# Q and K weights loaded three heads at a time, with another order of the work at both ends

## The chip, the cores and the metric

The kernel runs on one core of a Trainium2 chip. The metric is the device time of one execution in microseconds (us). Engine names are those of the profile: PE multiplies matrices, PEld loads its weights, DVE and ACT do elementwise work, POOL and SP mostly issue DMAs, POOL also small computations.

## The reference

Two kinds of layer, each run twice, A, B, A, B, on x of 2048 rows by 512, all in bf16:

```python
for s in range(n_seg):                     # 64 segments of 32 rows
    h = concat([mem, xs])                  # 8 rows of memory, 32 of the segment
    q, k, v = h @ Wq, h @ Wk, h @ Wv       # 32 heads of 128
    p = softmax(where(mask, q @ k.T * scale, -1e9))
    o = (p @ v) @ Wo
    mem = o[:8]; outs.append(o[8:])        # the memory goes on to the next segment
...
h = sigmoid(g) * u                         # B: g, u, down projection, F = 1792
```

Each layer takes a layer norm first and adds its input behind it. A starts from the same mem0 and the same weights both times. So the segments of one A are a chain: segment s + 1 needs the memory that segment s gives.

## The kernel before, in words

**Steps.** Both A layers run in one loop of 70 steps (emit_step). Step t does segment t of the first A layer and, beside it in the same matmuls, segment t - 6 of the second. The first six steps and the last six therefore have one layer alone (40 columns in a matmul, and not 80). Four segments are a block of 128 rows; when a block has left the first A layer, its B layer (ffn, lines 1048 to 1150) runs between the steps, and so on for the second. A step goes through 6 head groups: heads 0 to 2 and 16 to 18, then 3 to 5 and 19 to 21, and so on to 15 and 31. Per group: Q and K (L892), scores (L906), the softmax on DVE and ACT (L920 to L937), transposes (L949), P times V (L975), and the output projection (L993) into one PSUM bank for all groups. The next step needs the memory columns from that bank, copied at L1011.

**V.** V of the rows of x is not made in the steps. A V pass (v_pass, lines 686 to 711) takes 128 rows, makes V for eight pieces of 512 columns with four matmuls each (L695; I call these four a V piece), copies each out of PSUM, and stores it to a scratch tensor in DRAM; a step fetches its rows from there (L861). Seven passes at the start, 56 V pieces, serve ten blocks (v_group); their copies go to nine staging buffers, which are the B layer's weight tiles, not needed yet. A half pass (v_half, L732, stores at L746) and a strip (L817) do the same for a part of a block. In every step a strip makes V of the 8 memory rows and a few rows of x.

**Loads at the start.** All weights stay in SBUF. load_weights (lines 582 to 614) issues them on SP's queue: Wv in 8 pieces of 4 heads, the x of nine blocks between them, then Wq, Wk and Wo. Wo comes by head group. Wq and Wk come in pieces that start at heads 0, 3 and 9 (and 16, 19 and 25) and hold 3, 6 and 7 heads. In DRAM a head has 256 B in each of 512 rows, so a piece of m heads is 512 rows of 256 m bytes.

**What sets the order.** Each operation is a task with its engine, cost and keys read and written (Planner.add). SEQUENCE, a compressed list in the file, gives each task its place: at each moment an engine takes, of the tasks that are ready in a model of the chip, the one with the lowest place (forward, lines 272 to 413). What comes out is the program's fixed order on each engine; on the chip every engine takes its queue in order. Tasks that may run on either of two engines (copies on ACT or DVE, the boot stores on SP or POOL) get the one that is free first in the model. Where the model sees PE idle at either end, filler matmuls on a tile of zeros (L1218) go in.

Of the kernel before, what the change touches and what calls it, by code (L numbers as in the profile page):

```python
# [53 lines left out]
;Ag)rXk7pcfB%7A@!gH@5PER9zwFwU*Txh6(FIfkX|(7J?i&Gymhh!kX3<9*It9&+^ANuZ3nQF%vjb@k;)ADNDw~7A&yK6rftjYT<(0_Cu$F5_QL}_k&+#M$g4fMAuI3%VR%9II^4edG>hLecVFKKZ  # L54
fiq<zaDy4oUFv58J8W8}M`2{oi5UUb^!f*Ro0Ll?vc4MO@r^c`&wF^g&x{e8(wi=&1jnm{X}@GBNB?B98ftnN@q;Urg_TN7gRljNIZ1xL04!;{jd2yH$?cL&EwR4Y4Tqu8pK|P3tu<gW{h$`ab{UE_
fqK5_Bs&J*b^6-QBtiB1Rm-Zu8Nlc!2f&|gEyzQ&Zou|%s7^3{5zh9KTUR}tya8Oc6!P`{0)Vq8I;Cl`Bjt~AjrB%)CqD@z82Z2w;QrC0`{pXpx_R2Wh&&#2H3QIv3WnP|a@1!GQgacw;pKW^M`R|!
Nk+QQ;DjyYF5GF7!M*<sd8cVD>2uHyj70Z$6aD8lSDtqSMB#M+!9iZef2n{|jXj7clA2G^EzqM!g-lB)@}v+s<dLTg#Kii~);*dJP_OtPjOrD`dCRS`B*?af^G#|5&z)YMf)|%^UO;YbIwUZ94H|;|
&I8kZBVH%Vr|M`z4VQLMuW2mhCo%WGrCP@C3|aBQ!Z@sF?{dn1nHiX-Hcv2SE;6gPREA8v1gxUN5fjwov7s7E=){nUleMkl)rSwf-#NWnt+iLb)vYQSg8NO|ck6a&f5J`jCYy?w$`JBYrP7VoA#kkX
>yw8_VzTSGOpj8yq?_x;;hBH;rz~q4SdF9ZBg{rG@)htW>FtF!fG!q1a8hR)S^e6}q?Lzs^}+^#ob7fH!>Fyt6Ec%(XxD2g=*h~t0x*|HYIgpYBcJ&io_?o{l)`4GU_@%j@)8o~)(WjyR`I-_DVdEX
qpsq`mM61>+(8TaM-5>9Drz=jnb)-=yYKy|4I>K@zHNw@rcCC|=f*ye&WaMflMV5|xPNyTb*H)NgH9?jw1M*`|Aqy&^a*rUk;3mH)kGJznF1RvY3@t@=2^xaH0-f1Ty6gB5>G7cN@NTPLrchUmPhHP  # L60
BPzZ2ia}YU1q5^?Zh`JV^|-uLP^j5y#P_ZT06?ozV2jLQSp96AT@omT@9`T$m-yy@g4kD5^7&#?)KvIhz5<IDDn_B}S$w_%O54$*Uf&%*f!G9A0k)w2S80jRm_OzzD}%&|JCO=Jux2;jsV1&&*ocDe
vv19OW<}n=z=BXtevuQth?wJcFw3v~A;KU0Fj8U7v;-ubd1)6$LvOp^(EF2YN4lWzA>9UsIioM@psu~u&Horxi#{K)nGF~9<5jCnBT^6l!UsB(k4o)!8A~I>f8#r%yu%<R0mYyTfZ<)Sni2UT(vn0#
tm2cI5k@+Ojklj8V{nBRX$UB+gfBzr^hrH>$u5kX5;NqVjvk?&E^!9Un709~&!yGdZ`zS12GJ~~o>$PW0_Q(~(ech%@Dd4F?a@?s&4w?B3X^B#o>$WuxPHlU8E1h;6sRCPM;Cb&M89tcFI3Fc7SaL-
@ko8IZK`J@W2GEGmX}g(7vDTBKpV{0l0Fa*zKW5nQtSNYScG9m-W4oihEpRM9oZhx$s8@o43g~=;)6hTN^z^Shvggyiw$J(S&trHsZko5QCciufS!$?n=$+iEW_#~(`j}&V4WCWgYlK!d#Qs8!?9zj
+bqOxo_kt*eZ7rE@04&B0z8Nz9i<d40QttTz6^4LDi~8yhg8P4NzvULMSQJ-$b!TRs-7IAd_l8GT;#XHgZcX$-$b)HgDh{d9p!Ey5NK#kZ(Nzsu&svhey17&ct5)NozyL<4jW>hTpOmDH`UV?uNeKn
ulL27>(f<<fI2lD7P@{ZxKK5izxo4o_!^ec%pEaQr`~plAyRxTVWrISSzr8X5TfH(1GV1AzqFJC@ZL5V(+q2z_(&=mUZDhaes!D&m_4JvmfF?Tb1D<p2^ZH$QTP$`?ht%YJSK>L&CcqNEJ<!Kr{4oz
vj+K3Emf<Ch%)`ULp{|Z!2<pl7r@(XMSkbViiH_g;!i$l%ewSb&20V3maX%pZQ9=^qZ9wc+A{sGfKnIIgZi9N`Aj$1&p0a=tUVPau*9x6O+3z+=cQwW#v2L`O$oZv0t|=^q0+3wovlZqw;CjluSfY1
7;)b2dM;AEItw!IJo9aZVFG>~c1D!+Q8oJ6gHCVjgh+q=g5RV7n;S4Z{Vb-#GBbB5;S`h<JtFjk*+%dBbL|0-RP<JoBUp$?mRdco7QSmHHji-UX7~{&TCk0xhlix|OcNZzn$a?dwXxy6toswR3nCxg
<$l)jDf(|Z9;2QA2Pa?Sr*59(v?!>Gw*!qSrriD#k;zlQ3O)3BertDQxc3{@%R7C#_YLB_AsNpEq&sbpzKmH~RYP~bk{Zd_?;Wo1EPM{r9g$C}>3;0X_dxzhSf2(<dWtt@E+CAb_+p>QbPZxM{{PS3
*en5KD&!3JofsA3^5fe+Yc=aOqR)fM<|mNjpQ}L_L`b6F5Z9!0Ny_KiYa1f=>UfHv5NT}Dt#)}&@tB}*TmVzJN!1wQ308W#%Ewt9=zute@fBG_bJI~rE8@x(8H9zT)JiPkVik)hOISJpJ`Z|aqfuxS  # L70
9MY^{ThVokOpd=UmpouWZAyJ+>Q&s<TSe0J7BeE=BIr=gLszKqR~2v6Y6>hu2k+cm^UC_1#1b|?t!P7;XyfV~lp@ZnPb$}EWnWzg)_Pm2Q2jbtP7fuO#3di=k)6Dpo<n|F!K`{GgUY<TL&xEiPlsLE
&`&N90i`ZrB`F!^X2xQ#Z*X7g10f8gpm<n@MdGTPU@}*SmWq{(s7(9g_Cv(?{N1{2oaF^jfe$o_VK4qMF^xSK*{cee3e$;(u_$eW`lc&g&EI&y4i*uW%6zw-NX1hb(pOJBbt)zq^a*_i4QZU3OsA`a
ogk8T2n3iX4#2Ol?c4h;A1AqM9wA^Jr*lL?l6X!W4a}idB0|TS{P^F0xoo=H?n}?x#S)J57?AP`%qwl>;dln_?FWE@z$Yf>Vqz`|dwyR1uaTh&cJ&l`kd!X_?-X)Uh(;|b$81Dn>eA?1v=O~yq6@bR
lvtg%>-}E)I4o%t7|qUp0K%C@$IO_3Q8c<f2sy?3NQKPEsTbru3QRD|F$a4d@f{&HJW`|O6+dZE$zQ(5B{Er!7rj;f4B;-AE4MX{;f6HfmZJze6(XM=l9u^A_U!OD95{V?ww{=>wQP72Z~s4Qm*vR?
e*y&gf*;_)**=M^LbI7dC46mRe<kfr+>_l^QZ>lm(OXgC(MLi@qI+N!-8i=oU4&L8DE2q;wf%=IK%<}jzPwj}l6xHHB!-gZcv^HoZ{V!;w_?ExVSCPsDrsA{#Sb51#5b-20&?c^99>Nt=R8W4MSi*l
MCgAULe{=wE<IiLPE}6f&Z9CBTjxxm#$_7R6;Z-ebVg&LO>WXD!Pep6L3A0rMfMW?E%7v;VO`&f|Ap|wZ??;v^Q~wr_4FD&tZm<<vV<O6&>j+yJH$*U-MCo}`YUh|$58?UEU%S|;`YMe5WJlSWE_kL
E)LRM0MQ6r<a(5C^kO>B<W_mrR)FViX&=9@G;RSwumdZ&Qt1(0oIO6ak`3nRTF(wTL^pIe!t#dYVm=<rx<3Qr+huU{k!&q2AKPMS@{}fFPJPOl#O~xT)AjxxLZv|mhvohJ9z}-?!-FGN&=ldq)4r!D
*cp!V%Xw+RfahwLc)Ig{IHF)!SEG<NE#(9Yjhv#WJHTKEisY~5+qr=eRZhP)FaoF64N_9o35pnE(v8PoEVgW0r7x!jM^tenC7jjy!)MB3AcYWC48j5cMuv^}G6mD{UWyge2qtcY@;VQVZW$|axO~Oh
vJ(=-Q@Ew*P=dF|XXgO7`vJ<K48cKaSn5!FbYSw;t|wilbDVKhl?<VuNKghUS_lENW9>r$n!HW<BYwx!DFqn}AM7hQA@+s#m*u9N`b@Ma9m(V@dcecx`>pXpHMrdvT!$c6$7K*gPb#>jO6SUnwQF@S
>&t@I)gR?aZ}gYOy@|#4pu_GanAT5qv_jCS5Bv&znUe*1UBapE&|l`w?O1MdgnZ0R>Mw-E2=S@|2~OEKN1d=5kb0C<kwu$H!>xGujj568I8SGM7M8A~PmPpMktJ_zpry#uUGFxUxwuGjCr~0sf2+7g  # L80
1QQD+ok!zeEc-N#r4j85HjD_IIP7)bE0pBeVVwgpGLUF`aXcEYnas+nct*2CTatDY-UO860yp_D;wWRpnHqVob|AJG7Eu_;>7MspwFG-#th34g)A=(1$WWqkU;dyO*fYj89O$tHXy+9?G6n&!nE-bT
uHD2FL;P#J3)5yM(sJ4mXzUH7K%MW7ut6#aKE_VEm8Zy-<yJf7`JD;Ds5Y`Z;5r^JhiwaiY`Yzu+r<wjQ5Jo3qztp-Yaeftih>wiGv?Z>PImvDU$@!v+b{k6>d0r$Nyk>FDKbk@R8n3?EwnO2Jg_HM
^&{BYQ8~-q2UvBMkkT}=lF||tq88|}HA%Z!Mt#`v=86No_G8L~#*ll=e=mHZvdY}~2W}KZX>Q6&iLKNDoZhI7TM(m#F!*Py7hpHcsLyRcn)4c;_seEgk97w&NXraXv<}|Yrx`T)jmEs3KDJqcrl)v+
a`E{XIOU{=9wyfA_Qe6Fg7PICy+z0rWItXRiR_fcrE1b+YtfpKgby_i#DiZ#q>GE6gKJTEca-j*m_AZaS4r+{5`fIsD&Eka>#T$1h%?;0L<5{vRMqk<8KPEk@Hw2d(cY(lH4`Vc4`a4Z=uhAXua01S
d}N%2@j4-Sn=puE>7zRCBiN}PtDL0phD3sq=I<r8HJ|%r%nhYL7_BikjSVR7+}$I#^phFzOtMlRr9wvktyrcN>^S>5uX~y;KOZ)07B|Qpvfzi}nE<fV`fY&4nmh5Vo=gj<YM<Et2XL=k(Gfy+aAziY
!^T6yS=iPENu&kYb=FMz$XP>`DbpK9ox{*OWEvuP-dmBN%G*ZNlp2hSa77%g8H}Q_vPe%^C_Wp@)l$iHJrqj#=?~-%OjTBz7-kBg`I(xH^>eR@G<Em|wx>|WJt-xLE^W6up^P9~Kzun|byk~JEL#qF
UT%u3pg>u~N>iFXr84s{rky2t>t)1^hbyS|duHgv<R>(*@EcY|68IFb_x<JivX6sMv3lk=G4)l-D|&A(+awSm>pxhC=g<Ailb*)61+`*VtE_9f)yaAZnZx0`&xUz9Bi)0ndpC81IL=Fj>o}=}Ch^mD
a{YD<DQ#UfTxfqfn^-c6BC>YaC?R{qp)yf?p^3FV`^;lp-G8kVmKY3DqUL^S7g8+yJY4Vqq+(;q2YardKTJIIfSm;hAPuL(^{=YS2(t@2CS#O|s>c+=cuo2pLjY8Q$x#DV6Zej6Z6+s2Jao_#6eB^N
7a5P*6g-Zs{MHJT@<NVSs+drmT7C3uX>~(ur1;DdnN#UDYL?v7!!Fre<D_&r)ysX~u$jJpBXkHfi3^CbRQiN2#eVj4*Y&1Y9&Yd62}WPCU&?}1jk)^<;Xj%lk#*xH0J&?acOayDsi(r9Pg2arChoLZ
-c0{UkOgOWe7F;kG@*`6JA3Tn`bJM{0HY}ewITRwN+$1#PQS@f-e0GvY)0$_E>?k<uwxEv0N7%EmpAT;Pguj6d{Vby55>>*K-;Iy`XUw~a}xZd?9AV_f!CW0v1lx`Y@Mez3s_!eUd;`Q1*q_s7(F>=  # L90
4|BDtOk7rIPYp}7tPpCvbDyozSV)N#SL-t8I#V*{;CN%gQSVpsRe{_W<u{-?#aIGWPKK%H>**?-Ee>E?+#s+xtjt>}|33G7$N>I7i12j!u*RF%AAMnT$i@ZE-;Dgde8ZKEW37GCDnvi=le%JSa+G{n
+&Iei>EHmn=Fsxv|3C+uBlYDwTeYMZ&|8yf!>xC<lEgQzP+}DO)!F0Rf-DyHJ&<4G8eX2f+_P;6p&iv_V7UBs;C9F-9w+M|V%Dl{fMndP&kvo}d~iFsz7en-le9_u7*050e=zT3TWENVzx4zpe*EaN
E_R$wJ-6^dPSSK@HOiCva7<DlXkg9$A4q~qoev;f>xEG5`j|;}P6atT6JKHMeOBIUD!T7j@4=|Nf2Mg|DNFxWR&Hobs33JvVoFWbB(+u~7S$IxLqhyuGE&<vvl{CyO&z1oqHfh|2xyX5WdT^mjU{tL
qaiR6CykR9^~7dzlRAX3MnyC%)N&8XzzBT>bv5sR!f20Ha(j*RX9WbB&PIxchc5h=Fmjcqzgq1c{LF1WAx56-)nRxBt(DTxU^e<pf5p<J$)x~lc3BEtc>5LooO%n>XFGs~e{wNRGFTg$-_-?oHq5=9
w4PjSRCtdm*_=uiYlvVz!YpcU&k&0W4`R>fm7lQteSFF!M_52KaD|hF4CV}>6@KAW_}6k%yr)uH5D+@!u!nR>=?c#?EH^}0gd<j=cI~S7NNJIjZ-;~~8~e*@$)xkTbtoPX8<ePoaKkwZfMKsxKmi0a
GuEMV*kIW9?cN!r2{Z}sRkM}Hp5K)F0tm@-G^~vb{o~t{NOIx4)$8Ga?v>%CZ73bbqe-h(VGLXgCktybTz0o?*E>l{R4ioO9icVr#Jc5)aU&C~A(1}LPak#aaOk$ttY*Q>Q>`CmI4~tQH4Rm@q>AcG
?R9df05%CgU-Pl14SM+nGMMPk&7`&ID>$|s48-otrEtg9kZZs)L+Zk9Nq1c>2IhbA`rKc1L|lOdv395d@BqQ!ZW)c&jT3=)jt-4AomSOAN>}-+7UgX$PQR8kPkU=(C_~M3H8RWgDI*wT6%5ZSNsgs^
@`+tryad9d!c$`q7#<gIBN`WEv|-=;q=6=-NNKI5N(Z+cjzi^+wN~=rb_XnLICCEjg{eVEW=&t+zXa@WrA38tA1)DC&=s`b`b6z{%beoMIYj(s$g%D*K;Hz;p&*5f%6hl7ZLwiUm$bqc=)TbL>Z(9z
# [360 lines left out]
class Kern:  # L459
# [123 lines left out]
    def load_weights(self):  # L583
# [21 lines left out]
        for heads, us in self.groups:  # L605
            n = len(us)
            for nm, sb, v in (("wq", self.wq, wq_v), ("wk", self.wk, wk_v)):
                for h0 in heads[:2]:
                    m = parts.get(us[0])
                    if m:  # L610
                        cs = slice(h0 * P, (h0 + m) * P)
                        ld(sb[:, :, cs], v[:, :, cs], P * self.DC * m * P * 2, [(nm, h) for h in range(h0, h0 + m)])
# [685 lines left out]
```

## Time and profile before

| what | value |
|---|---|
| three runs | 1783.15, 1783.18 and 1782.39 us, median 1783.15 |
| profiled execution | 1783.15 us, of which 1781.3 us span |
| granted TensorE clock | 1.000 |
| PE busy | 1754.0 us of the span |
| DMA moved | 270.66 MB, 26.53 MB of it in the first 85 us |
| DMA share, 20 to 85 us | 0.92 |
| DMA share, 85 to 101 us | 0.28 |
| V pieces (L695) busy, 20 to 85 us | 42.98 us on PE |

The span goes from the first to the last instruction. A busy PE counts matmuls of any use, filler too. A DMA share is the mean busy share of 16 DMA engines; it can pass 1, since packets of one engine overlap. Times in a timeline are us from the span's start.

### The profile page before, as it was taken

The page shows a single profiled execution, that of the slowest core. Times are in us where ns is not written, and L with a number is a line of the kernel's source. Part 1 is how long each engine was busy: PE and PEld are TensorE (multiplying, and loading weights), DVE is VectorE, ACT ScalarE, POOL GpSimd, SP SyncE. Part 2 cuts the span into 40 slices and gives each one's busy share as a digit, 9 for nine tenths or more (in the row PEclk, how much of TensorE's full clock was granted, in tenths as well). Part 3 has the DMA queues.
Part 4 walks back from the last instruction along what each step waited for, and adds up shares of the span by engine and source line. Part 5 has one row for each costly group of instructions (what it writes and reads, how often), then busy time and mean ns, then how long its engine had stood idle before and what let it go on. Part 6 is the DMA issues. An engine that isn't in the chain of part 4 may idle for free.

```text
span 1781.3 us, 91977 instructions
## 1 busy us (share of the span) xinstructions
PE 1754.0 (98%) x39873; PEld 1517.1 (85%) x40083; DVE 1144.1 (64%) x3931; ACT 1167.8 (66%) x2973; POOL 573.8 (32%) x828
## 2 busy tenths in 40 slices
PE   9999999999999999999999999999999999999998
PEld 4688888888888898989898898988888888989886
DVE  4376666776577666756666676657656665666675
ACT  6676666666666666666766666666666766667564
POOL 5314031513233242323324241333324232333332
PEclk9999999999999999999999999999999999999999
DMA  9825254635555464445546453555555454555543
GB/s 342 265 74 165 59 155 121 195 105 158 146 162 153 133 174 136 139 137 165 160 130 198 135 161 106 154 160 167 156 148 172 111 145 140 158 156 139 165 143 94
DMA packets 131943, 270.66 MB, mean 152 GB/s; under 512 B 30394, under 2 KB 65090, under 8 KB 131538
## 3 DMA queue, kind: packets, MB, share of 16 engines
q0 software_dynamic: 56240, 181.91, 34.7%
q1 hardware_dynamic: 75298, 82.86, 16.3%
q8 instruction: 314, 5.14, 1.3%
q14 instruction: 91, 0.75, 0.1%
HBM read 220.41 MB, written 25.69 MB: 138 GB/s over the span
## 4 chain that ended last, share of the span: by engine, by line
PE 91%; DVE 5%; ACT 2%; issue 1%; DMA 1%; SPq 1%; POOL 0%; ACTq 0%; DVEq 0%; POOLq 0%
PE bank L892 31%; PE bank L993 17%; PE bank L1095 11%; PE bank L695 8%; PE bank L817 7%; PE bank L975 4%; PE bank L906 4%; PE bank L1119 4%; PE bank L949 2%; DVE st L920 1%; PE bank L1218 1%; PE bank L664 1%; DVE small L925 1%; DVE small L932 1%; DVE st L927 1%
## 5 line engine op out<-in xcount | busy, mean ns | idle before, releaser
L892 PE MATMUL bank<-hT,wq_sb 128*128 128x80 bf16 (+1 forms) x8960 | 622.6, 198 | 1.3 <-issue 0.6
L892 PE MATMUL bank<-hT,wk_sb 128*128 128x80 bf16 (+1 forms) x8960 | 622.5, 198 | 0.6 <-issue 0.6
L1232 ACT CAST qku<-bank 128x480 bf16<-128x480 f32 (+3 forms) x770 | 388.3, 512 | 222.5 <-PE bank L892 142.0
L892 PEld LDWEIGHTS <-wq_sb 128*128 128x128 bf16 x8960 | 454.1, 99 | 35.0 <-issue 25.1
L892 PEld LDWEIGHTS <-wk_sb 128*128 128x128 bf16 x8960 | 450.8, 99 | 0.8 <-issue 0.7
L920 DVE TENSOR_TENSOR st<-bank,cst 40x240 f32<-40x240 f32 (+3 forms) x768 | 277.7, 367 | 200.9 <-PE bank L906 194.2
L993 PE MATMUL bank<-otsb,wo_sb 128*128 128x80 bf16 (+1 forms) x8960 | 362.8, 198 | 1.9 <-ACT otsb L1232 0.2
L993 PEld LDWEIGHTS <-wo_sb 128*128 128x128 bf16 x8960 | 336.7, 99 | 16.3 <-issue 1.9
L1087 POOL DMA_DIRECT2D wg<-in_B_w_gate_dram x217 | 164.0, 756 | 299.1 <-PE bank L1095 109.8
L1232 ACT CAST otsb<-bank 128x480 bf16<-128x480 f32 (+3 forms) x420 | 199.8, 482 | 59.6 <-PE bank L975 47.6
L1088 POOL DMA_DIRECT2D wu<-in_B_w_up_dram x217 | 163.9, 756 | 197.3 <-PE bank L1095 89.3
L1113 POOL DMA_DIRECT2D wd<-in_B_w_down_dram x217 | 153.8, 709 | 213.4 <-PE bank L906 74.5
L930 ACT ACTIVATE st<-st 80x240 f32<-80x240 f32 (+3 forms) x420 | 159.5, 381 | 39.9 <-DVE st L927 37.1
L654 POOL TENSOR_TENSOR small<-small,cst 128x1 f32<-128x1 f32 (+1 forms) x80 | 44.8, 562 | 413.7 <-DVE small L653 410.2
L1095 PE MATMUL bank<-xnT,wg 128*128 128x128 bf16 (+2 forms) x1784 | 172.0, 219 | 0.8
L1095 PE MATMUL bank<-xnT,wu 128*128 128x128 bf16 (+2 forms) x1784 | 171.2, 219 | 0.0
L906 PE MATMUL bank<-qku 128*128 128x80 bf16 (+1 forms) x2240 | 161.0, 198 | 1.5 <-ACT qku L1232 0.2
L932 DVE TENSOR_REDUCE small<-st 80x6 f32<-80x240 f32 (+3 forms) x420 | 150.6, 360 | 16.3 <-ACT st L930 14.0
L937 DVE TENSOR_TENSOR pb<-st,small 80x240 bf16<-80x240 f32 (+3 forms) x420 | 153.6, 368 | 4.2
L927 DVE TENSOR_TENSOR st<-st,small 80x240 f32<-80x240 f32 (+3 forms) x420 | 154.1, 368 | 3.1
L925 DVE TENSOR_REDUCE small<-st 80x6 f32<-80x240 f32 (+3 forms) x420 | 151.4, 362 | 4.6
L975 PE MATMUL bank<-ptsb,vsb 104*128 104x80 bf16 x2048 | 140.2, 199 | 3.0 <-DMA vsb<-sst 1.5
(102 smaller groups left out, 2345.2 us busy)
## 6 DMA issues: line engine op xcount, KB each, us to landing
wg<-in_B_w_gate_dram POOLq DMA_DIRECT2D x220, 256.0 KB, 4.3
wu<-in_B_w_up_dram POOLq DMA_DIRECT2D x220, 256.0 KB, 4.3
wd<-in_B_w_down_dram POOLq DMA_DIRECT2D x220, 256.0 KB, 4.3
vsb<-scr SPq DMA_DIRECT2D x460, 48.0 KB
vsb<-sst SPq DMA_DIRECT2D x464, 32.0 KB
scr<-vst SPq DMA_DIRECT2D x112, 96.0 KB
wv_sb<-in_A_Wv_dram SPq DMA_DIRECT2D x8, 512.0 KB
wo_sb<-in_A_Wo_dram SPq DMA_DIRECT2D x10, 384.0 KB
```

Of the source, the lines that this page charges most:

```text
L892: nc.tensor.matmul(o_ap, lhsT=W[:, c, h * P:(h + 1) * P], rhs=mv(c), start=(c == 0), stop=(c == DC - 1))
L906: nc.tensor.matmul(s_all(SB)[:, w0 + i, :], lhsT=fview(qku[:, i, 0, 0:1], [(1, P)]), rhs=qku[:, i, 1, 0:ncol], start=True, stop=True)
L920: pl.add("DVE", dve_ns(n, True), lambda gsz=gsz, hs=hs, st=st, SB=SB, pj_=pj_, npj_=npj_, mk=mk, idx=idx: nc.vector.tensor_tensor(out=st[p ...
L925: pl.add("DVE", dve_ns(n), lambda hs=hs, st=st, mx=mx: nc.vector.tensor_reduce(out=mx[pr, hs], in_=st[pr, hs], axis=AX.X, op=ALU.max), r=s ...
L927: pl.add("DVE", dve_ns(n), lambda gsz=gsz, hs=hs, st=st, mx=mx: nc.vector.tensor_tensor(out=st[pr, hs], in0=st[pr, hs], in1=mx[pr, hs].uns ...
L932: pl.add("DVE", dve_ns(n), lambda hs=hs, st=st, sm=sm: nc.vector.tensor_reduce(out=sm[pr, hs], in_=st[pr, hs], axis=AX.X, op=ALU.add), r=s ...
L975: nc.tensor.matmul(fview(OB[:, o:o + 1], [(ncol, 2), (1, L)]), lhsT=self.vsb[halves[u // 8]][0:64 + L, j, (u % 8) * P:(u % 8 + 1) * P], rh ...
L993: nc.tensor.matmul(WB[:, c * ncol:(c + 1) * ncol], lhsT=self.wo[:, h, c * P:(c + 1) * P], rhs=otsb[:, hl, 0:ncol], start=(h == 0 and c == ...
L1087: pl.add("POOL", 760, lambda wg=wg, fs=fs: nc.gpsimd.dma_start(out=wg[:], in_=self.wgv[:, :, fs]), r=[("wo", self.H - 1)], w=[gk] + bt, la ...
L1088: pl.add("POOL", 760, lambda wu=wu, fs=fs: nc.gpsimd.dma_start(out=wu[:], in_=self.wuv[:, :, fs]), r=[("wo", self.H - 1)], w=[uk] + bt, la ...
L1095: nc.tensor.matmul(gu[:, 2 * i + k, 0:n], lhsT=W[:, c, i * P:(i + 1) * P], rhs=xnT[:, c, rw], start=(c == 0), stop=(c == DC - 1))
L1232: nc.scalar.copy(out=dst, in_=src)
```

## The change

The pieces of Wq and Wk follow the head groups: 3 heads each, and one head for the last group. 12 loads on SP become 24; the bytes stay.

```diff
-        parts = {0: 3, 3: 6, 9: 7}
         for heads, us in self.groups:
             n = len(us)
             for nm, sb, v in (("wq", self.wq, wq_v), ("wk", self.wk, wk_v)):
                 for h0 in heads[:2]:
-                    m = parts.get(us[0])
-                    if m:
-                        cs = slice(h0 * P, (h0 + m) * P)
-                        ld(sb[:, :, cs], v[:, :, cs], P * self.DC * m * P * 2, [(nm, h) for h in range(h0, h0 + m)])
+                    cs = slice(h0 * P, (h0 + n) * P)
+                    ld(sb[:, :, cs], v[:, :, cs], P * self.DC * n * P * 2, [(nm, h) for h in range(h0, h0 + n)])
```

SEQUENCE is replaced. The half pass stores V by row first and segment second in both kernels; the diff doesn't touch it. Both lists can be read as tasks: 13280 before, 13292 after. Without the 24 and 36 loads of Wq, Wk and Wo they hold the same tasks, in the same places from step 7 to step 62 and from step 67 on. They differ in the first 1220 places, by up to 120, and in steps 63 to 66, by up to 26. Some places, those loads left out of the count:

| | before | after |
|---|---|---|
| head of SP's list | Wv 4, Wv 0, x3, x4, x1, x8, x2 | x2, Wv 4, x4, Wv 0, x3, Wq 9, x1 |
| first x to be normed | blocks 3, 4, 2 | blocks 2, 4, 3 |
| last Q or K piece | 285 | 312 |
| its head group in step 0 | 337 to 345 (heads 3 on) | 368 to 372 (heads 12 on) |
| last piece of Wo | 385 | 395 |
| last Wo matmuls of step 0 | 452 | 456 |
| strip of step 1 | 461 | 462 |
| V pieces ahead of that strip | 54 of 56 | 55 of 56 |

Wv 4 is the piece from head 4 on, x3 the x of block 3. The last pieces of one head stand in the after list at places 157 (Wk 15), 223 (Wk 31), 274 (Wq 15) and 342 (Wq 31), these with the loads counted.

## The prediction

> **What bounds the kernel now.** I read the page first (busy shares, the slices with the granted clock, the chain that ended last), then the chain in order of time for both ends, then busy time by stage, then the DMA by window.
>
> ```profile
> PE 1754.0 (98%) x39873; PEld 1517.1 (85%) x40083; DVE 1144.1 (64%) x3931; ACT 1167.8 (66%) x2973; POOL 573.8 (32%) x828
> PE 91%; DVE 5%; ACT 2%; issue 1%; DMA 1%; SPq 1%; POOL 0%; ACTq 0%; DVEq 0%; POOLq 0%
> ```
>
> PE carries 91% of the chain; the clock is granted in full throughout. The change alters no matmul, so the time can move only where PE waits or runs filler matmuls (L1218, on a tile of zeros). Those alone, by stage (the first columns are the stretch, its length and PE busy):
>
> ```profile
> 0.00:20.00 20.00, 12.82 (x50) 5.20 (x50) 1.00 0.95 309
> 20.00:85.00 65.00, 0.54 (x2) 0.15 (x2) 1.00 0.92 313
> 85.00:101.00 16.00, 1.03 (x4) 0.33 (x4) 1.00 0.28 80
> 101.00:118.00 17.00, 2.50 (x11) 0.89 (x12) 1.00 0.29 80
> 118.00:134.00 16.00, 2.27 (x10) 0.55 (x7) 1.00 0.27 72
> ```
>
> To 12 us PE has nothing to do: x and Wv are on the way. From 14 to 85 us it has hardly any filler, because the V pieces of ten blocks stand between the pieces of step 0, while DMA is full (last columns: share 0.92, 313 GB/s). From 85 us on DMA is nearly idle and PE has holes: steps 1 to 3 are one layer alone, and their chain through DVE and ACT is longer than their matmuls. So two things can cost time: PE waiting before 85 us for a weight that comes late, and a V piece used up before 85 us that would have filled a hole after it.
>
> **Term 1, the order on PE.** The chain about the end of step 0:
>
> ```profile
> 81.24 0.81 PE bank L695 x3
> 82.05 0.80 PE bank L993 x32
> 82.85 0.87 PE bank L695 x4
> 83.72 1.84 PE bank L817 x32
> 85.56 2.51 PE bank L892 x96
> ```
>
> L993 is the last Wo of step 0, L817 the strip of step 1, L892 its Q and K; L695 is V. One V piece of four matmuls is 0.86 us. In the list of before 54 of the 56 boot pieces stand ahead of the strip of step 1, in that of after 55. PE takes its queue in order and is full here, so step 1 starts 0.86 us later, and the piece is missing behind it, in steps where a filler takes its place. Bounds: 0, if the chain of step 1 ran through that piece (the chain view shows two L695 pieces there, at 92.63 and 93.70 us), and 0.86. I take **+0.86**.
>
> **Term 2, the head of SP's queue.** The first V piece needs the x of blocks 3 and 4 in both lists. Before, two Wv pieces and these two go first, 2 x 0.52 + 2 x 0.13 = 1.31 MB; after, the x of block 2 goes ahead as well, 1.44 MB. At the 346 GB/s of 6 to 7 us this is 0.38 us, and PE is full from there on. It could also be a gain: the x of block 4 now has one Wv piece ahead and not two, and the layer norms are a series on DVE (the first starts at 6.29 us after 5.20 us of waiting for an x). Bounds -0.5 and +0.5, one issue on SP (0.5 us each there); I take **+0.4**.
>
> **Term 3, rows of Q and K.** A row is one head's 256 B times the heads of the piece. Before: 6144 rows, of 768, 1536 and 1792 B. After: 12288, of which 10240 of 768 B and 2048 of 256 B. The bytes stay. What a row costs comes from two stretches of 11 us in which DMA is full, 15 to 26 us (mostly 768 B and 1 KB rows) and 35 to 46 us (mostly 1.5 to 1.8 KB):
>
> ```profile
> DMA packets 4031, 3.88 MB, mean 353 GB/s; under 512 B 267, under 2 KB 3882, under 8 KB 4030
> ```
> ```profile
> DMA packets 2836, 4.34 MB, mean 394 GB/s; under 512 B 276, under 2 KB 2558, under 8 KB 2834
> ```
>
> Each is 16 x 11 = 176 us of engine time. With a fixed price a for a packet and b bytes per ns: 4031a + 3.88 MB/b = 2836a + 4.34 MB/b, so 1195a = 0.46 MB/b; put back in, b = 30.9 and a = 12.5 ns. The other bound is the whole queue of SP:
>
> ```profile
> q1 hardware_dynamic: 75298, 82.86, 16.3%
> ```
>
> 16.3% of 16 x 1781.3 us over 75298 packets is 61.7 ns for 1100 B, less 1100/30.9 leaves 26 ns. The change adds 6144 rows and 16 completion packets for each of 12 more DMAs, 6336: at 12.5 ns **4.95 us** of all 16 engines, at 26 ns 10.3 us, and 0 if rows in flight hide the price. I take 12.5, since it comes from the stage itself.
>
> Two things take it up. First, DMA is not full all the way (column before the last: share):
>
> ```profile
> 45.00:50.00 5.00, 4.95 (x27) 2.38 (x27) 0.14 (x1) 3.36 (x6) 3.54 (x7) 1.00 0.98 357
> 50.00:55.00 5.00, 4.95 (x72) 3.10 (x72) 2.69 (x8) 3.06 (x6) 1.77 (x4) 1.00 0.75 235
> 55.00:60.00 5.00, 4.98 (x27) 2.25 (x26) 1.13 (x2) 3.01 (x6) 2.76 (x5) 1.00 0.91 282
> ```
>
> (0.02 + 0.25 + 0.09) x 5 = 1.8 us are free there, since SP stands behind V stores that wait for ACT, with the next weights behind them. After, weight loads stand at those places. Lag left: 3.15 us. Second, cover. The last K pieces go out at 54.58 us, and SP's queue thins out after 66 us (60 to 66, then 66 to 70):
>
> ```profile
> 54.58 1.99 SPq L591 DMA_DIRECT2D wk_sb<-in_A_Wk_dram  x2
> ```
> ```profile
> q1 hardware_dynamic: 1330, 1.79, 83.0%
> ```
> ```profile
> q1 hardware_dynamic: 518, 0.50, 47.4%
> ```
>
> So they have landed at about 66.5 us; PE uses them at 69.6. That is 3 us of cover. In the list of after the last K and Q pieces stand some 25 places later and their users 25 to 30 later: the cover stays. The last Wo goes out at 72.8 us and is used at 81.9. A lag of 3.15 under 3 us costs PE about nothing, **0 to 0.2**. If the cover is gone, all 4.95 us stand on the path. What is late next are the V stores in the same queue: nine staging buffers hold them, and ACT already waits 0.6 us for such a store (ACT wu waiting for DMA scr from wg). I double that: **+0.6**. SP's 12 more issues at about 0.6 us are 7 us beside queue waits of 11.1 us for PE and 12.9 us for ACT and DVE copies at the strips: 0, and up to +5 if stores get stuck behind loads.
>
> The 256 B rows have no twin in the trace. By the fit one is 12.5 + 256/30.9 = 20.8 ns, inside the 4.95; if it cost as much as the mean packet, 61.7 ns, 2048 of them add 5.2 us. I keep the fit, and the other end for the range.
>
> The Trainium skill, "DMA: Bandwidth & Descriptors", section Specifications, asks for at least 512 B for line rate and says that shorter ones are read, modified and written. No run here shows a load of 256 B rows yet; if that doubled their time, it would be an estimated 2.7 us more. The same page, section Bandwidth, would batch to 1 MiB and more, and gives 138 GB/s at 64 KB against 341 at 1 MB. The trace speaks against using that rate here: with pieces of 384 and 512 KB in flight together 15 to 26 us runs at 353 GB/s. By the page's rates the pieces of 384 KB would lose more than the rows do.
>
> **Term 4, the end.** Places differ in steps 63 to 66 by at most 26, with the same work. Filler from 1640 us on is 0.82 + 0.97 + 1.30 + 3.41 = 6.5 us; most lies behind 1740 us, where the lists agree. What the other order moves is a share of the 3.1 us ahead of 1740: **0**, bounds -1 and +1.
>
> **Sum.** 0.86 + 0.4 + 0.6 + 0 = +1.9 us. The profiled execution took 1783.15 us (1781.3 of span, 1.85 around it), which is also the median. Forecast: **1785.0**. About 0.2%, 3.6 us, is what a measurement of this kernel can tell from no change, so this counts as within 0.2%; its own range is 1782.5 to 1786.7.
>
> **Rivals.**
> 1. Weights late (slower). The extra packets stay on the path: cover is used up, and PE, in order, stands at the late head groups of step 0 with V pieces behind it that can't overtake. From 4.95 us of uncovered lag and the 0.86: 1789.0; with dear 256 B rows or packets of 26 ns, above 1791. It decides as soon as 2.3 us of the lag come through, that is when the cover is 0.8 us and not 3. For it: DMA at 0.92 over the whole stage, filler at only 0.54 us, so nothing soaks up a wait. Against: 3 us of cover and 1.8 us of free DMA. Chance 0.34.
> 2. Nothing happens. Rows are hidden, orders are worth the same: 1783.2. For it: equal work, and a list equal from step 7 to 62. Against: the moved V piece. Chance 0.12; it too lies within 0.2%.
> 3. Faster. The finer pieces let the first heads come earlier and the first x arrives ahead of Wv: if the wait for the first x (5.20 us) fell by the 3 us that one MB of Wv takes at 346 GB/s, and the end gave 1 us, 1779.2. Against: the first V piece still needs block 3, behind both Wv pieces. Chance 0.08.
>
> **Chances.** Forecast 0.46, rivals 0.34, 0.12, 0.08: within 0.2% 0.58, slower 0.34, faster 0.08. The range leaves out the far ends of rivals 1 and 3: 1781.5 (all lower bounds of terms 1, 2 and 4) to 1789.5 (rival 1 at 4.95 us, and a bit of the dear rows).
>
> **What would show it.** Right: the strip of step 1 (L817) between 84.5 and 86 us and not 83.7; DMA share 0.95 and more between 45 and 60 us; some 6300 packets more on SP's queue, with 2000 more under 512 B; filler before 85 us unchanged but for the head, and 0.9 us more from 85 to 118 us. Wrong: PE idle between 60 and 85 us, or that strip after 87 us (rival 1); the first V matmul before 13 us (rival 3); filler behind 1640 us other than 6.5 us by more than 1 (term 4).

## The result, and the profile after

| | before | after |
|---|---|---|
| median | 1782.77 us (1782.01 to 1783.18, 4 runs) | 1791.58 us (1789.16 to 1792.57, 4 runs) |
| profiled execution, span | 1783.15, 1781.3 us | 1791.99, 1790.2 us |
| granted TensorE clock | 1.000 | 0.998 |
| packets on SP's queue | 75298 | 81602 |
| packets under 512 B, all queues | 30394 | 32634 |

The ratio is 1.0048, 95% interval 1.003 to 1.0065: slower by 8.8 us, outside the range of the prediction (forecast 1785.0, range 1781.5 to 1789.5).

All the loss is at the start. The strip of step 1 begins at 83.72 us before and at 93.52 us after, 9.8 us later; the last instruction on DVE ends 9.2 us later. In between the lag is 10.6 to 11.0 us from step 6 (170.22 us after) to about 570 us and then shrinks to about 9 in steps, with the same order on both sides; I have no explanation for that part.

Line numbers after are two lower than before (L693 is a V piece, L815 a strip, L890 Q and K, L991 Wo, L592 a weight load, L1226 a boot store, L1230 a copy on ACT, L1216 filler). The page of after, engines and chain:

```profile
PE 1758.6 (98%) x39874; PEld 1518.0 (85%) x40085; DVE 1145.5 (64%) x3943; ACT 1164.7 (65%) x2961; POOL 573.7 (32%) x828
PE 85%; DVE 6%; issue 3%; DMA 2%; SPq 2%; ACT 2%; POOL 0%; DVEq 0%; ACTq 0%; POOLq 0%
```

PE is busy for longer with the same matmuls, because some ran at a lower clock, and it lost 6 points of the chain. Filler (L1216) by stage, columns as in the prediction:

```profile
20.00:85.00 65.00, 0.00 (x0) 0.00 (x0) 0.97 0.93 289
85.00:101.00 16.00, 0.00 (x0) 0.00 (x0) 0.89 0.55 178
101.00:118.00 17.00, 2.54 (x10) 0.77 (x10) 1.00 0.24 67
```

There is no filler up to 101 us, the clock is below 1 (the column of 0.97 and 0.89), and 289 GB/s were moved where it was 313. The chain about the end of step 0:

```profile
83.14 8.21 DMA wo_sb<-in_A_Wo_dram
...
91.39 0.42 PE bank L991 x8
91.81 1.71 PE bank L693 x4
93.52 2.55 PE bank L815 x19
```

The last Wo now ends a wait: it was issued at 83.1 us (72.8 before), landed at 91.4, and PE waited for it. The V piece behind it takes 1.71 us and not 0.87, since the clock is low there. So weights are late, which is how rival 1 ends. What made them late shows on ACT and SP, between 36 and 68 us. The timeline of ACT; in brackets how long ACT stood, and for what:

```profile
37.55 0.68 ACT L1230 CAST wd<-bank 128x512 bf16<-128x512 f32 x1
44.52 0.59 ACT L1230 CAST wu<-bank 128x512 bf16<-128x512 f32 x1 [6.28 <-DMA scr<-wu]
...
62.33 0.58 ACT L1230 CAST wu<-bank 128x512 bf16<-128x512 f32 x1 [5.96 <-DMA scr<-wu]
```

And that of SP:

```profile
37.57 2.84 SPq L592 DMA_DIRECT2D wk_sb<-in_A_Wk_dram  x2
46.59 0.56 SPq L1226 DMA_DIRECT2D scr<-wd  x1
```

The sums of ACT's waits of that kind from 20 to 100 us, before and after (us in all, times, longest):

```profile
ACT wu L1232 <- DMA scr<-wg: 0.6, 2, 0.3
ACT wu L1230 <- DMA scr<-wu: 12.2, 2, 6.3
```

ACT stands twice for 6 us at a copy into the staging tile wu, until a store from wu has landed (12.2 us in all, and 0.6 before). From 40.4 to 46.6 us SP issues nothing: its next instruction is a boot store whose copy sits behind the waiting one on ACT, and the remaining weight loads are behind that store. What it does to PE, its clock and DMA, in slices of 2.5 us (columns: stretch, length, then busy time of PE, PEld, DVE, ACT, POOL, then clock, DMA share, GB/s):

```profile
45.00:47.50 2.50, 2.19 (x12) 1.13 (x13) 0.00 (x0) 2.50 (x7) 0.62 (x2) 1.00 0.26 85
60.00:62.50 2.50, 0.93 (x4) 0.29 (x3) 0.00 (x0) 0.17 (x1) 0.00 (x0) 1.00 0.96 279
65.00:67.50 2.50, 2.50 (x7) 0.91 (x6) 0.00 (x0) 1.39 (x3) 0.78 (x2) 0.50 1.08 351
```

DMA runs empty at 45 us (0.26), PE stands at 60 to 63 us since ACT doesn't empty the PSUM banks, and then runs at half the clock. PE's timeline has the wait:

```profile
62.96 5.30 PE L693 MATMUL bank<-wv_sb,xvf 128*128 128x512 bf16 x16 [2.04 <-ACT wu L1230]
```

### The profile page after: what moved, and what is told of

Same layout as the page of the kernel before. It is cut to its first block, busy times and chain, and to the rows that moved or that the text cites. A ratio compares the mean times of both kernels' runs of the same rounds, so it can differ in the third digit from the quotient of the medians.

```text
span 1790.2 us, 92001 instructions
## 1 busy us (share of the span) xinstructions
PE 1758.6 (98%) x39874; PEld 1518.0 (85%) x40085; DVE 1145.5 (64%) x3943; ACT 1164.7 (65%) x2961; POOL 573.7 (32%) x828
## 2 busy tenths in 40 slices
DMA packets 138263, 270.66 MB, mean 151 GB/s; under 512 B 32634, under 2 KB 71426, under 8 KB 137858
## 3 DMA queue, kind: packets, MB, share of 16 engines
q1 hardware_dynamic: 81602, 82.79, 16.3%
## 4 chain that ended last, share of the span: by engine, by line
PE 85%; DVE 6%; issue 3%; DMA 2%; SPq 2%; ACT 2%; POOL 0%; DVEq 0%; ACTq 0%; POOLq 0%
PE bank L890 29%; PE bank L991 16%; PE bank L1093 10%; PE bank L815 7%; PE bank L693 6%; PE bank L973 4%; PE bank L1117 4%; PE bank L904 4%; PE bank L947 2%; DVE st L918 2%; PE bank L1216 1%; DMA wo_sb<-in_A_Wo_dram 1%; SPq L592 1%; PE bank L662 1%; DVE small L923 1%
## 5 line engine op out<-in xcount | busy, mean ns | idle before, releaser
L890 PE MATMUL bank<-hT,wq_sb 128*128 128x80 bf16 (+1 forms) x8960 | 622.8, 198 | 1.4 <-issue 0.6
L890 PE MATMUL bank<-hT,wk_sb 128*128 128x80 bf16 (+1 forms) x8960 | 622.4, 198 | 0.8 <-issue 0.8
L1230 ACT CAST qku<-bank 128x480 bf16<-128x480 f32 (+3 forms) x770 | 387.9, 512 | 221.7 <-PE bank L890 143.2
L890 PEld LDWEIGHTS <-wq_sb 128*128 128x128 bf16 x8960 | 454.4, 99 | 34.6 <-issue 24.3
L890 PEld LDWEIGHTS <-wk_sb 128*128 128x128 bf16 x8960 | 450.7, 99 | 1.0 <-issue 0.9
L991 PE MATMUL bank<-otsb,wo_sb 128*128 128x80 bf16 (+1 forms) x8960 | 363.6, 198 | 3.2 <-DMA wo_sb<-in_A_Wo_dram 1.6
L991 PEld LDWEIGHTS <-wo_sb 128*128 128x128 bf16 x8960 | 337.1, 99 | 18.6 <-DMA wo_sb<-in_A_Wo_dram 1.8
L1230 ACT CAST otsb<-bank 128x480 bf16<-128x480 f32 (+3 forms) x420 | 199.6, 482 | 59.6 <-PE bank L973 48.3
```

The source lines that it names most:

```text
L890: nc.tensor.matmul(o_ap, lhsT=W[:, c, h * P:(h + 1) * P], rhs=mv(c), start=(c == 0), stop=(c == DC - 1))
L991: nc.tensor.matmul(WB[:, c * ncol:(c + 1) * ncol], lhsT=self.wo[:, h, c * P:(c + 1) * P], rhs=otsb[:, hl, 0:ncol], start=(h == 0 and c == ...
L1230: nc.scalar.copy(out=dst, in_=src)
```

## The experiments

Each was timed beside runs of the kernel before on the same chip. The medians of before differ by up to 3.3 us from one group of experiments to another (1781.02 to 1784.35), so the ratios count. The lists are told in words in the diffs below, since SEQUENCE is compressed.

**First question: loads, or order?** The theories were the packets (rival 1), the mere number of loads, and the list. For these four kernels before took 1781.49 us.

*Only the list of the end.* The kernel before, with SEQUENCE that of after from the middle on, so in steps 63 to 66:

```diff
 SEQUENCE: places up to the common middle as before
-          places behind it as before
+          places behind it as after
```

> Kernel before with only the end of the list (steps 63 to 66) taken from after; loads and start as before. If the loss is made at the start, as all of the rows, the order and the count theories say: 1782.8 us, within 1 us. If the new order at the end takes part: 1784 or more.

1781.42 us, ratio 1.0002 (0.9993 to 1.0011). The end costs nothing that can be told. The start of this kernel is that of before, and yet its strip of step 1 begins at 84.75 us, against 83.72 in the profile of before: a difference of 1 us in that place says nothing.

*Only the pieces.* The 24 loads of after, in the list of before, each small piece at the place of the large one that it was part of:

```diff
 SEQUENCE: as before, but
-  wq3 (6 heads)                wq9 (7 heads)
+  wq3 wq6 (3 each)             wq9 wq12 (3 each) wq15 (1)        # wk and the upper heads alike
```

> Pieces of three heads (24 loads, 12288 rows), list of before, each large piece replaced on the spot by its two or three small ones. Rows theory (shorter rows make the full DMA stage longer): 4.95 us of packets and the waits they set off, 1788 to 1792. Count theory (12 more issues on SP and more transfers in flight): 1786 to 1792 too. Order theory (the list of after is what loses): within 2 us of before, 1781 to 1785.

1783.50 us, ratio 1.0008 (0.9999 to 1.0017), strip of step 1 at 85.41 us. ACT waits for a store three times, 0.3 us each. The packets are all there and take at most 0.17%: rival 1's mechanism falls as the cause of the loss.

*Only the order.* The large pieces of before in the list of after, each where its first part stands there (Wq 9 a little later, behind the x of block 13):

```diff
 SEQUENCE: as after, but
-  wq3 ... wq6                  wq9 ... wq12 ... wq15
+  wq3 (6 heads)                wq9 (7 heads)
```

> Pieces of three, six and seven heads as before, list of after at both ends; a large piece stands at the earliest place of its small ones (Wq 9 behind the x of block 13). Order theory: 1788 or more, with ACT waiting some 6 us for a staging buffer. Rows and count theories: within 2 us of before, 1781 to 1785.

1792.01 us, ratio 1.0062 (1.0048 to 1.0075), strip at 94.92 us, and ACT's two waits for a store from wu are there with 10.8 us together. The list of after makes the whole loss, with large pieces as well, and since its end costs nothing, it is the start of the list.

*The number of loads.* The list and the long rows of before, but large pieces split by blocks of 128 rows into as many loads as after:

```diff
-                        ld(sb[:, :, cs], v[:, :, cs], ...)
+                        for i, (a, z) in enumerate({3: ((0, 4),), 6: ((0, 2), (2, 4)), 7: ((0, 2), (2, 3), (3, 4))}[m]):
+                            ld(sb[:, a:z, cs], v[:, a:z, cs], ...)
```

> 24 loads with the rows of before (6144 of 768, 1536 and 1792 B): the large pieces are split by the 128-row blocks of the weights and not by heads; list of before, the parts on the spot. Count theory: as the pieces of three in that list, 1786 to 1792. Rows theory: within 2 us of before, 1781 to 1785. Order theory: the same.

1782.04 us, ratio 1.0007 (0.9998 to 1.0016), strip at 85.03 us. The count costs nothing that can be told from no change. (The opposite, as few loads with short rows, was not tried.)

**Second question: what in the order?** A list changes the order on every queue. The waits point to one thing in it. A staging tile holds a pair of V pieces, k and k + 1. The planner asks for a free tile at the task that was *added* first (users[0], piece k, line 260 of before, in plan). Where a list runs piece k + 1 first, nobody asks; which tile it is gets settled when piece k comes, and tells only that the tile is free by *then*. Worked out from the plans, this is common: 15 of 28 pairs before, 14 of 28 after. It does harm only where the tile that is picked was stored from a moment ago. Before has luck: its shortest time from the issue of the last store from a tile to the next copy into it is 2.7 us, the next one 8.9. After has two short ones, with piece k more than 7 us behind piece k + 1 in both. In the plan of after, piece k + 1 is copied into wu2 at 35.69 us, 0.3 us behind the issue of the last store from it (35.38), and in a later pair at 52.87 us, 3.5 us behind (49.42). On the chip the first of these stores went out at 37.97 us and landed at 44.42, and ACT waited for it. The plan of the version with only the order has two such places as well (0.6 and 3.3 us). The planner knows nothing of that wait, and puts its span at 1768.2 us for after and 1769.1 for before.

Theory: this early refill makes the loss. Rival: the order of SP's queue, with Wo and the small pieces too late in it. The test is to change tiles and no order. Where nothing else is said, before took 1781.02 us beside these kernels.

*After, tiles chosen anew.* Behind the plan each pair gets the tile that was stored longest ago:

```diff
         order = self.pl.plan()
+        T = self.pl.tasks
+        bs = [bf for bf in self.pl.bufs if bf.pool is self.bootp and bf.users]
+        first = lambda bf: min(T[u].start for u in bf.users if T[u].on != "PE")
+        last = [0.0] * 9
+        for bf in sorted(bs, key=first):
+            bf.slot = last.index(min(last))
+            last[bf.slot] = max(T[u].start for u in bf.users)
```

> The kernel after, every engine's order, all loads and all weights pieces as they are; only the tile that each pair of V pieces is staged in is chosen anew, behind the plan: always the one whose last store was issued longest ago. In the plan the shortest time from a tile's last store issue to the first copy that refills it goes from 0.3 and 3.5 us to 9.9 us. Theory of the staging tile (ACT stands for two stores from a tile that is refilled at once, and all that is late follows from it): ACT's two waits of 6.3 and 6.0 us at the copies into wu vanish (under 1.5 us together), the strip of step 1 is back from 93.5 to 84 to 87 us, time 1781.5 to 1785, ratio 0.999 to 1.0015. Rival, the order of SP's queue (Wo and the last small pieces stand too late in it, behind stores): strip still at 91 or later, 1788 or more, ratio 1.003 or more. If both share it: between.

1781.51 us, ratio 1.0002 (0.9993 to 1.001). The chain's line for the strip, and the slices of above:

```profile
84.11 1.84 PE bank L815 x32
```
```profile
45.00:47.50 2.50, 2.45 (x12) 1.18 (x12) 0.36 (x1) 1.62 (x4) 0.13 (x1) 1.00 1.08 392
60.00:62.50 2.50, 2.50 (x16) 1.01 (x18) 0.00 (x0) 1.71 (x4) 0.00 (x0) 1.00 1.07 368
65.00:67.50 2.50, 2.50 (x16) 1.20 (x15) 1.79 (x5) 1.85 (x4) 0.97 (x2) 1.00 1.08 373
```

Every queue has the order of after, the loads are those of after, and the loss is gone: DMA is full at 45 us, PE doesn't stand, the clock stays. The rival falls.

*After, only the first early refill taken out*, by exchanging two tile names (wu2 and wu0, numbers 8 and 6) from 35 us of the plan on:

```diff
+        for bf in bs:
+            if first(bf) > 35000.0:
+                bf.slot = {8: 6, 6: 8}.get(bf.slot, bf.slot)
```

> The kernel after, same orders and loads; from the pair at 35.7 us of the plan on, two staging tiles change names, so that the first of the two early refills (0.3 us behind the store's issue) has 7.1 us, and the second (3.5 us) stays. Theory of the staging tile: ACT's wait of 6.3 us near 44 us goes, one of 4 to 6 us near 60 us stays; strip of step 1 at 87 to 91 us, time 1784 to 1789, so about half of the loss. Rival, SP's order: as after, 1790 to 1792.5. Rival, the first wait alone makes the loss: 1781.5 to 1784.

1781.06 us, ratio 1.0001 (0.9992 to 1.001), strip at 83.50 us. I had expected half of the loss to stay. The second early refill is still in the plan, but its wait doesn't come: on the chip its copy begins at 56.69 us, after a wait for PE, and the second wait of after was due to the lateness that the first had made.

*After, only the second taken out*, the same with names 8 and 5 from 52 us on. Before took 1784.35 us beside it:

> The kernel after, orders and loads as they are; two staging tiles change names from 52 us of the plan on, so that only the second early refill (the one of 3.5 us) goes, to 7.1 us. The first, of 0.3 us, stays. If the first wait starts the loss and the second only follows from its delay: the wait of about 6 us at 38 to 45 us stays, none over 1 us after it, time between 1783 and 1788; with the second wait's 6 us and the low clock behind it gone it should be nearer to before than to after. If the first wait makes the whole loss by itself: 1788 to 1791 on the scale of before at 1781 to 1783.

1789.92 us, ratio 1.0031 (1.002 to 1.0042). The first wait is there with 6.2 us, later ones of 1.4 us. The bulk of the loss, 5.6 of 8.8 us, comes with the first wait alone, near the upper edge of what I gave for that case. The chain:

```profile
81.93 7.94 DMA wo_sb<-in_A_Wo_dram
...
91.15 1.84 PE bank L815 x32
```

Wo is late by itself, without a second long wait on ACT: the path goes over SP, which stood for 6 us with the loads behind it. A piece of Wk was late as well: PE stood for 2.24 us for it, up to 71.44 us.

*Before, with early refills put in.* Orders and loads of before; two exchanges of tile names (wg0 and wd1 from 37 us on, wg0 and wd2 from 53 us on), so that a pair is copied 0.9 and 1.4 us behind the issue of the last store from its tile:

```diff
+            if first(bf) > 37000.0:
+                bf.slot = {3: 1, 1: 3}.get(bf.slot, bf.slot)
...
+            if first(bf) > 53000.0:
+                bf.slot = {3: 2, 2: 3}.get(bf.slot, bf.slot)
```

> The kernel before, every order and load as it is; at two places of the plan (37.2 and 53.0 us) two staging tiles change names from there on, so that a pair is staged in a tile whose stores were issued 0.9 and 1.4 us earlier. Theory of the staging tile: ACT gets two waits of 4 to 7 us for a store at such a copy, the strip of step 1 goes from 83.7 to 89 to 95 us, time 1787 to 1792, ratio 1.003 to 1.006, without any change in the weights or in the order of a queue. Rival, order of SP's queue or of the weights: nothing to lose here, 1781 to 1784. Middle: if the loss needs the finer loads as well, waits are there and the time stays under 1785.

1786.19 us, ratio 1.0029 (1.0018 to 1.004). The chain:

```profile
36.34 10.39 DMA scr<-wd
46.83 0.59 ACT wd L1241
...
88.09 1.84 PE bank L817 x32
```

The fault alone makes the kernel before 5.2 us slower, without a change to weights or to any order. That is a little under what I had expected (1787 and more, strip at 89 or later). ACT stood for 8.7 us at the first refill and 1.6 at the second; one store took 10.4 us from issue to landing, with DMA at 1.05. The execution in this profile took 1784.32 us, 3.3 above before, and has no stretch of low clock; six of the seven have one by their mean clock (0.998 or 0.999).

*Before, tiles chosen anew.* Its own plan has one early refill (2.7 us):

> The kernel before, orders and loads as they are, staging tiles chosen as in the version of after above (the one stored longest ago). Its plan has one early refill, 2.7 us behind the store's issue, for which ACT waits at most 0.3 us by its trace. Theory of the staging tile: nothing or up to 0.6 us gained, 1781 to 1783.5, ratio 0.999 to 1.0005; strip of step 1 at 83 to 84 us.

1780.43 us, ratio 0.9997 (0.9988 to 1.0006), so no gain that can be told: before loses nothing measurable to its tiles.

*The planner mended.* In after, the tile is asked for at the piece that runs first; every task keeps its engine, place and time in the plan, only tiles differ. Beside before at 1784.35 us:

```diff
-            T[bf.users[0]].acq.append(bf)
...
         assert not left
+        for bf in self.bufs:
+            if bf.users:
+                T[max(bf.users, key=lambda u: T[u].tail) if len(bf.pool.tiles) == 9 else bf.users[0]].acq.append(bf)
```

> The kernel after with the planner mended: the free staging tile is asked for and taken at the V piece of a pair that has the lowest place in the list, not at the one that was added first. The plan comes out with the same order, engine and time for every task; only tiles differ. Theory of the staging tile: as the version with tiles chosen anew, ACT's waits for stores under 1 us each, strip of step 1 at 83 to 85 us, ratio 0.999 to 1.0012. Rival, that the loss came from a low clock that some builds get by chance: anything up to 1.005.

1782.65 us, ratio 0.9996 (0.9986 to 1.0005), strip at 83.31 us, waits for stores 0.3 and 0.4 us, clock 1.000 in all ten executions. The mended planner picks the same tile for every pair as the version with tiles chosen anew above; by their plans the two are one program. So this shows that the mend in the planner is enough, and repeats that result beside other runs, but it is no further case: two different programs with the order and loads of after have no loss, this one and the one without the first early refill.

*Before, one early refill late in the stage.* Names wg1 and wg0 exchanged from 76.5 us on (0.7 us behind the issue). Before took 1784.35 us beside it:

> The kernel before, all orders as they are; two staging tiles change names from 76.5 us of the plan on, so that the pair at 76.8 us is staged in a tile whose last store was issued 0.7 us earlier. Gap as short as in the version of before with two early refills, where a store took 10.4 us and cost 5.2 us, but at a place where DMA begins to run empty (share 0.91 at 75 to 80 us, 0.23 behind it) and few V pieces are left. If the price of an early refill is the time that a store needs in a full DMA: ACT's wait under 4 us and 0 to 2.5 us in time (1781 to 1784.5, strip of step 1 at 83.7 to 86). If any early refill costs the same: 4 us and more, strip at 88 or later.

1788.96 us, ratio 1.0024 (1.0014 to 1.0033), strip at 89.4 us. ACT's timeline, then the slices:

```profile
83.01 0.58 ACT L1238 CAST wg<-bank 128x512 bf16<-128x512 f32 x1 [3.65 <-DMA scr<-wg]
```
```profile
80.00:82.50 2.50, 0.83 (x32) 0.73 (x29) 0.24 (x1) 0.00 (x0) 0.00 (x0) 1.00 0.43 148
82.50:85.00 2.50, 0.95 (x38) 0.95 (x38) 1.14 (x6) 1.35 (x5) 0.00 (x0) 1.00 0.00 0
85.00:87.50 2.50, 2.50 (x32) 1.40 (x29) 0.73 (x3) 0.84 (x4) 0.00 (x0) 0.52 0.07 13
```

Here my theory of the price was wrong. The wait was shorter, as said (3.65 us), but the time rose by 4.3 us by the ratio (4.6 between the medians) and not by 0 to 2.5. Behind the copy on ACT were the softmax and the copies of the last head groups of step 0; PE, in order, stood for 3.2 us at a Wo matmul that waits for such a copy, its next V piece came behind that at 85.6 us, and the clock fell on top. A short wait at a tight place can cost nearly as much as a long one under cover.

## Why the prediction was wrong, point by point

**Term 3, the step that failed:** "nine staging buffers hold them, and ACT already waits 0.6 us for such a store ... I double that: +0.6". ACT waited 12.2 us. I scaled a wait of the old order, as if it depended on how full DMA is. It depends on which tile a copy goes to, and that the list decides anew. Read from the list, the question would have been: for each tile, how long after the issue of its last store does the next copy into it come? The answers 0.3 and 3.5 us stand in the plan of after, against 6.4 to 6.5 us that stores from wu on POOL's queue took to land between 36 and 46 us, and 8.7 us for the store behind the second wait. The same term allowed "up to +5 if stores get stuck behind loads". What came was the reverse: loads stuck behind a store that waited for ACT. The term had even seen this queue ("SP stands behind V stores that wait for ACT, with the next weights behind them"), but counted it as free DMA time.

**The rest of term 3 held.** 6304 packets came (6336 predicted), 2240 of them under 512 B. A packet of 256 B took 18 ns (median; the fit said 20.8), so it is not as dear as the mean packet (61.7), and its time did not double either. By the packet records of the traces all rows of Q and K together took 381 us of engine time before and 431 with only the pieces changed: 3.1 us of all 16 engines, where 4.95 was written down. With tiles chosen anew the DMA share from 20 to 85 us is 0.98 and not 0.92; the added work of the rows went into the free share, as the term said, along with some 0.5 MB more that was moved in that stretch. The pieces alone cost at most 0.17%. The cover was there too: with the tiles chosen anew the last Wo goes out at 75.2 us (72.8 before) and PE waits for no weight. In after the 6 us in which SP issued nothing ate it.

**Rival 1 named the right place and the wrong cause.** Weights were late, PE was idle between 60 and 85 us and the strip came after 87 us, its signs. Its "above 1791" for dear packets was met by luck. Its cause, extra packets, costs nearly nothing; the cause was a wait on another engine's queue, two queues away from the loads.

**Term 1 and 2, seen without the fault.** With the first refill taken out the V piece is indeed missing behind: filler from 85 to 118 us is 5.03 us and not 3.53 (0.9 more was expected). But the strip isn't later by anything that can be told, 83.50 against 83.72 us; 0.54 us of filler in 20 to 85 us and 0.57 in the first 20 us went away, which may be why. Together the terms gave nothing that can be measured, where +1.3 us was written down.

**Term 4 held:** 0, by the run with the end alone; filler behind 1640 us is 1.79 + 4.72 = 6.51 us in after, 6.51 before.

**Where the 8.8 us are.** From 35 to 95 us PE is busy for 53.68 us in after and for 59.12 with tiles chosen anew: 5.4 us of standing. The clock below 1, (0.08 + 0.26 + 0.34) x 5 us in three slices of 5 us, is 3.4 us more. The sum is 8.8 us; the strip is 9.4 us later than in that version, so some 0.6 us stay open, and it is partly chance that the sum equals the difference of the medians. That the low clock follows from standing is argued, and was not tested by itself. For it speak the time order and the mean clock: 1.000 in every execution of before and of all versions without a long stand of PE, 0.998 or 0.999 in all 25 executions of after, of the order alone, of the second refill taken out and of the late refill, and in six of seven of before with early refills.

No version here beats the kernel before beyond what can be told: the best ratios are 0.9996 and 0.9997, with intervals that hold 1.

## What to carry to other kernels

When an order is replaced, check what a planner takes for granted about it, here that the first-added user of a buffer runs first; a list that breaks it can give a program with waits that the plan doesn't contain. That an older list broke it without harm is no proof: before broke it as often and had luck with its tiles. For every reused buffer, read from the plan the time between the issue of its last store and its next write, and compare it with how long stores take to land in that stage of the trace. A wait is priced by what stands behind it on its engine and by who waits for that, not by its own length or by the mean of such waits in the old order.

## What the runs showed of the hardware that was not expected

A stand of PE seems to cost more than itself. In after PE stood from 60.92 to 62.96 us, and from 64.2 to 67.6 us the granted clock was half (0.50 in the slice shown); a matmul of 512 columns took up to 635 ns and not 378. A second such stretch of 3.4 us came at 91.5 us, behind two shorter stands (1.03 us up to 90.17, 0.56 us up to 91.39). Each costs about 1.7 us: two in after, one in the run with the second refill taken out (0.58 and 0.73 at 72.5 to 77.5 us) and one in the late refill (0.52 and 0.80 at 85 to 90 us). In the run with only the order changed PE stood for 3.85 us up to 65.39 us, and the half clock lasted twice as long, 6.8 us from 64.6 us on. It is not certain, though. In the profiled execution of before with early refills PE stood for longer than in after, and the clock stayed at 1.00, while six other executions of that kernel have a mean clock of 0.998 or 0.999:

```profile
47.47 2.75 PE L695 MATMUL bank<-wv_sb,xvf 128*128 128x512 bf16 x12 [3.57 <-ACT wd L1241]
```

The Trainium skill, "TensorE: Matmul & The Clock Gate", section "Part 1: The HAM clock gate", says that the clock halves after an idle window of about 3.4 us, returns after as long a busy one, and that the window runs freely. The 3.4 us at half clock agree with that, and so does the chance in it. That a single stand of 2.04 us, or two of 1.03 and 0.56 us with work between them, can come ahead of a fall, and one of 3.57 us without any, is what the runs here add.
